# Gates of the first six tiles by a matrix product in a fused attention and mixture-of-experts kernel

## The chip, the cores and the metric

The kernel runs on one core of one Trainium2 chip. The metric is the device time of one execution in microseconds (us), the median over runs; lower is better. "The profile" is one execution taken by the hardware profiler, with the page and the trace made from it. Engines are named as there: PE does matrix products (PEld its weight loads), DVE and ACT the elementwise work, POOL the indirect transfers, and SP issues plain transfers; a q behind a name is that engine's instruction queue.

## The reference, cut to what matters

```
x   = chunked attention over q, k, v and memory rows      # 3072 tokens x 512
x   = soft mixture of experts of x                         # combine weights c (3072 x 32) times slot outputs (32 x 512)
noisy = x @ w_gate + log1p(exp(x @ w_noise)) * noise       # 3072 x 8
top2  = the two largest of noisy per token
w     = exp(top2 logits - their max) / (their sum + 1e-9)
out = zeros
for e in range(8):                                         # 512 -> 1024 -> 512
    out[tokens of e] += w[token, e] * (relu(x[tokens] @ w1[e]) @ w2[e])
```

## The kernel before

The kernel has three parts in one program. **Attention** (`attention`) and the soft experts' product (`soft`) run first; `soft` ends with the 32 x 512 slot outputs `po`, copied to SBUF as `so` (one half by ACT, one by DVE), transposed to `SOT`. **The last part** (`experts`) never forms x itself: a token's x is its row of combine weights times the slot outputs, so a gathered row of `table` (DRAM, 72 columns: 64 with the split combine weights, 8 with the token's gate for each expert) stands for a token, and the first layer of expert e is one matrix `G[e]` (128 x 1024), made by `prep_gs` from `SOT` and w1[e]. The second layer's weights are split into f16 high and low parts by `prep_hi` (ACT) and `prep_lo` (DVE), scaled by factors from `prep_s`, which need a maximum over w2[e] (`bound`, `bound_s`) and over the first layer (`prep_gmax`, `prep_row`, `prep_all`).

Tokens are worked in tiles of 128, six tiles per expert (`T0` = 6, `NTL` = 48), so tiles 0 to 5 are expert 0. For tile i:

- `gather(i)` (POOL, indirect): 128 rows of `table`, by the token indices `idx[:, i]`, into `CG[i]`
- `ct(i)`: transpose on PE and copy by ACT; `l1(i)`: eight matmuls, then HI = relu as f16 (ACT) and, by `lo(i)`, the remainder LO (DVE)
- `l2(i, ...)`: three groups of eight 128x512 matmuls, named by a number: 0 is HI with high weights, 2 is HI with low weights, 1 is LO with high weights
- `gate(i)`, `yv(i)`: the gate GW and the scaled copy y out of PSUM (ACT); `put(i)`: y is added to the rows of `out` by an indirect transfer on POOL

Indices of expert 0 are made first, by an early count of its tokens: a mask `s0`, its prefix sums, then `spread` builds the one-hot `oh_0` (24 blocks, 128 x 128 f16) and `ov` (block numbers times token values), and `inverse` multiplies them (24 matmuls) to `pv0`, which `decode` turns into `idx[:, 0:6]`. The other experts' indices follow later from all counts (`bases`, `positions`, `columns`, `invert`). Gates come from the top-2 choice (`top_max`, `top_eq`, `top_oh`: one-hots `oh`; `d`: difference of the two logits; `w12`: the two weights; `wd`: token by expert). As tiles 0 to 5 are gathered before `wd` exists, `wd` goes to a second DRAM table `gtab` as well, and `gates(i)` gathers from that; tiles 0 and 1 are copied from PSUM unscaled and multiplied in place by `rescale`.

`out` is cleared by four transfers of a quarter each (`zeros`), issued by SP; `load_e(1, 0)` and `load_e(1, 1)` load w1 and w2 of expert 1 (2 MB each, four transfers). All plain transfers named here go through SP's queue in the order in which they are written.

The order on each engine is the program order, written by hand. After the ramp (tiles 0 and 1, lines 703 to 808) a loop over `seq` does tile n, with the first layer of tile n+1 ahead of the second layer of tile n, and with the preparation of the next expert spread over the tiles by `plan`, `mid` and `ahead`.

Of the kernel before, what the change touches and what calls it, by code (L numbers as in the profile page):

```python
# [9 lines left out]
F32 = mybir.dt.float32  # L10
# [4 lines left out]
OP = mybir.AluOpType  # L15
# [110 lines left out]
def tile_kernel(ctx, tc, q, k, v, mem_k, mem_v, phi, sw1, sw2, wg, wn, noise, mw1, mw2, cf_in, c16_in, out):  # L126
# [9 lines left out]
    table = dr.tile([N + ND, ROW], F32, name="table")  # L136
    gtab = dr.tile([N + ND, E], F32, name="gtab")
    bp = ctx.enter_context(tc.tile_pool(name="bp", bufs=1))
# [5 lines left out]
    with ExitStack() as sctx:  # L144
# [44 lines left out]
        with ExitStack() as fctx:  # L189
            fw = fctx.enter_context(tc.tile_pool(name="fw", bufs=1))  # L190
            ft = fctx.enter_context(tc.tile_pool(name="ft", bufs=1, side="right"))
            tabs = [ft.tile([128, NT // 2, ROW], F32, name=f"tab{z}") for z in range(2)]
            ps = fctx.enter_context(tc.tile_pool(name="ps2", bufs=1, space=PSUM))
            for m in range(4, 11):
                for x in range(4):
                    load_w(m, x)

            def next_load(m, x):
                if 2 <= m < 7:
                    load_w(m + 9, x)  # L200

            rw = [t.rearrange("p (k d) -> p k d", k=n) for t, n in zip(raw, (4, 8))]

            def first_load():
                for t, src in ((rw[1], mw2), (rw[0], mw1)):
                    n = t.shape[1]
                    for x in range(4):
                        k = slice(x * n // 4, (x + 1) * n // 4)
                        nc.sync.dma_start(t[:, k, :], src[0].rearrange("(j p) f -> p j f", p=128)[:, k, :])

            def bounds():
                first_load()
                bound(nc, rw, big, s4, 0)
                bound(nc, rw, big, s4, 1, True)

            soft(tc, nc, phis, L, C, CT, SOT, zt, table, gtab, K, WT, next_load, bounds, tabs, fw, ps)
    with ExitStack() as ectx:
        rt = ectx.enter_context(tc.tile_pool(name="rt", bufs=1))
        ew = ectx.enter_context(tc.tile_pool(name="ew", bufs=2))
        ps = ectx.enter_context(tc.tile_pool(name="ps3", bufs=1, space=PSUM))  # L220
        experts(tc, nc, C, CT, SOT, sog, wgn, nz, zt, table, gtab, mw1, mw2, out, K, K16, rw, s4, big, rt, ew, ps)

# [16 lines left out]
def soft(tc, nc, SIT, L, C, CT, SOT, zt, table, gtab, K, WT, next_load, first_load, tabs, fw, ps):  # L239
    identf = K["ident"]  # L240
# [55 lines left out]
    for z in range(2):  # L296
        nc.sync.dma_start(table[z * N // 2:(z + 1) * N // 2].rearrange("(t p) c -> p t c", p=128), wrs[z])
    for t, w in ((table, ROW), (gtab, E)):
        nc.sync.dma_start(t[N:N + ND].rearrange("(t p) c -> p t c", p=128),
                          zt[:, None, 0:w].to_broadcast([128, ND // 128, w]))  # L300
    so = fw.tile([128, DM], F32, name="so")
    nc.scalar.activation(so[:, :DM // 2], po[:, :DM // 2], AF.Copy)
    nc.vector.tensor_copy(so[:, DM // 2:], po[:, DM // 2:])
    pt = ps.tile([128, 4, SL], F32, name="pd", bufs=1)
    for j in range(4):
# [3 lines left out]

def experts(tc, nc, C, CT, SOT, sog, wgn, nz, zt, table, gtab, mw1, mw2, out, K, K16, rw, s4, big, rt, ew, ps):  # L310
    spare = C.rearrange("p t s -> p (t s)")[:, F // 2:]
# [253 lines left out]
    prep_all(0, 0, 1)  # L565
    top_max(1)
    prep_s(0, 0, 1)
    for x in range(4):
        prep_hi(0, x)

    CG, CTT, HI, LO, RG, GT, GG, GW, YV, P2, PI = ({} for _ in range(11))

    def gather(i):
        CG[i] = ew.tile([128, ROW], F32, name="cg", bufs=7)
        c = GCOL(i)
        nc.gpsimd.indirect_dma_start(out=CG[i], out_offset=None, in_=table,  # L576
                                     in_offset=bass.IndirectOffsetOnAxis(ap=idx[:, c:c + 1], axis=0))

    def gates(i):
        GG[i] = ew.tile([128, 8], F32, name="gg", bufs=3)  # L580
        nc.gpsimd.indirect_dma_start(out=GG[i], out_offset=None, in_=gtab,
                                     in_offset=bass.IndirectOffsetOnAxis(ap=idx[:, i:i + 1], axis=0))
# [147 lines left out]
    nc.vector.reciprocal(w12[:, 0], w12[:, 0])  # L730
    tt(w12[:, 1], w12[:, 0], d, OP.mult)
# [639 lines left out]
```

## Time and profile before

| | |
|---|---|
| median of 3 runs | 554.92 us (554.15 to 556.75) |
| the profiled execution | 553.13 us, its span 551.3 us |
| PE busy | 483.7 us, 88% of the span |
| DVE, ACT, POOL busy | 324.3, 262.0, 258.3 us (59%, 48%, 47%) |
| chain that ended last | PE 67%, of it 40% line 666 (`l2`) |
| DMA | 111.34 MB, 202 GB/s over the span |

The span runs from the first to the last instruction that the profile holds. The part that the diff touches begins near 194 us, when the last matmuls of `soft` end, and reaches to about 275 us, when the loop over tiles has its regular rhythm.

### The profile page before, as it was taken

Reading aid. Unit: us, or ns where it says so; the run is one execution under the profiler, and the core shown is the slowest. Engines: PE = TensorE matmul, PEld = TensorE weight load, DVE = VectorE, ACT = ScalarE, POOL = GpSimd, SP = SyncE. Lnnn points to the kernel's source line nnn. Section 1 sums busy time; section 2 is a strip of 40 time slices with the busy share of each in tenths; the row PEclk is TensorE's granted clock in tenths of the full one; section 3 lists DMA queues with packets and bytes.
Section 4 is the critical chain, followed back from the end, with each engine's and each line's share of the span. In section 5 each row is a group of like instructions: output and inputs, shape, how many; then the busy total and the mean of one; then the engine's idle time right before and its main releaser. Section 6 shows DMA issues by size and latency. Waiting matters only on the chain.

```text
span 551.3 us, 12206 instructions
## 1 busy us (share of the span) xinstructions
PE 483.7 (88%) x4781; PEld 268.3 (49%) x4781; DVE 324.3 (59%) x725; ACT 262.0 (48%) x460; POOL 258.3 (47%) x312
## 2 busy tenths in 40 slices
PE   4799999997878872959899999999999999999990
PEld 3667667664424341424444454445544544545540
DVE  6799999999622046667656656563584565642110
ACT  4888888882112052236625346264272552642310
POOL 5988878781030004035733636355335464463241
PEclk9999999999999965898999999999999999999996
DMA  8799998869999999974593966748757673344352
GB/s 194 201 252 236 245 241 227 228 206 358 413 357 410 411 339 372 272 306 60 122 281 45 270 143 198 197 68 200 191 152 166 161 200 48 45 60 63 39 65 36
DMA packets 90161, 111.34 MB, mean 202 GB/s; under 512 B 43392, under 2 KB 55840, under 8 KB 90096
## 3 DMA queue, kind: packets, MB, share of 16 engines
q1 hardware_dynamic: 76944, 94.03, 53.6%
q0 software_dynamic: 9648, 16.20, 20.0%
q10 hardware_dynamic: 3504, 0.25, 0.5%
q8 instruction: 40, 0.66, 0.5%
q14 instruction: 25, 0.20, 0.1%
HBM read 89.21 MB, written 21.25 MB: 200 GB/s over the span
## 4 chain that ended last, share of the span: by engine, by line
PE 67%; ACT 8%; DMA 8%; issue 6%; DVE 5%; POOL 3%; ACTq 0%; POOLq 0%; DVEq 0%
PE l L666 40%; ACT big L1041 4%; PE tr L1031 4%; PE st L1055 4%; PE l L638 3%; DMA out_dram<-y,C 3%; PE av L1101 2%; PE g L369 2%; DMA w<-in_moe_w_dram 2%; DMA big<-in_moe_w_dram 2%; PE po L267 1%; PE p L253 1%; PE xt L1124 1%; ACT qT L1041 1%; PE xt L1138 1%
## 5 line engine op out<-in xcount | busy, mean ns | idle before, releaser
L666 PE MATMUL l<-big,hi 128*128 128x512 f16 x768 | 175.7, 381 | 0.1
L692 POOL DMA_INDIRECT out_dram<-y,C x52 | 87.6, 1685 | 140.7 <-ACT ctt L600 90.8
L648 DVE SCALAR_TENSOR_TENSOR lo<-l,hi 128x1024 f16<-128x1024 f32 x50 | 61.2, 1224 | 116.6 <-ACT hi L640 109.2
L666 PEld LDWEIGHTS <-hi 128*128 128x128 f16 x768 | 72.8, 98 | 84.2 <-issue 4.8
L683 ACT ACTIVATE y<-l,gw 128x512 f32<-128x512 f32 x48 | 32.8, 684 | 144.9 <-PE l L666 136.9
L666 PE MATMUL l<-big,lo 128*128 128x512 f16 x384 | 92.2, 383 | 0.0
L576 POOL DMA_INDIRECT cg<-table,C x50 | 54.2, 1085 | 48.4 <-DVE big L531 29.0
L666 PEld LDWEIGHTS <-lo 128*128 128x128 f16 x384 | 37.9, 99 | 45.0 <-issue 1.6
L1008 POOL COPY big<-big 32x768 f32<-32x768 f32 x64 | 56.5, 882 | 3.7
L640 ACT ACTIVATE hi<-l 128x1024 f16<-128x1024 f32 x50 | 51.2, 1024 | 3.5 <-issue 1.8
L1041 ACT ACTIVATE qT<-tr 64x384 f32<-64x384 f32 x64 | 34.3, 536 | 13.5 <-PE tr L1031 12.9
L433 DVE SCALAR_TENSOR_TENSOR big<-w,C,big 128x1024 f16<-128x1024 f32 x32 | 39.9, 1279 | 1.3 <-issue 1.1
L1031 PE MATMUL tr<-cf,big 128*128 128x128 f32 x192 | 30.3, 298 | 7.6 <-DMA cf<-in_const_f_dram 4.5
L429 ACT ACTIVATE big<-w,C 128x1024 f16<-128x1024 f32 x32 | 35.4, 1148 | 0.9 <-DVE C L405 0.7
L1041 ACT ACTIVATE big<-tr 64x384 f32<-64x384 f32 x64 | 32.9, 514 | 4.8 <-PE tr L1031 3.9
L1055 PE MATMUL st<-big,qT 128*32 128x128 f32 (+2 forms) x768 | 28.5, 284 | 5.1 <-ACT big L1041 3.2
L638 PE MATMUL l<-ctt,big 128*128 128x128 f16 x384 | 29.7, 221 | 3.0 <-ACT ctt L600 2.6
L1101 PE MATMUL av<-big,aT 128*32 128x130 f32 x768 | 27.9, 278 | 3.3 <-PE at L1086 2.1
L1013 POOL COPY big<-big 24x768 f32<-24x768 f32 x32 | 26.3, 824 | 9.5 <-DMA big<-in_v_dram 8.2
L1031 PEld LDWEIGHTS tr<-cf,big 128*128 128x128 f32 x192 | 22.2, 149 | 14.1 <-DMA cf<-in_const_f_dram 4.5
L638 PEld LDWEIGHTS <-big 128*128 128x128 f16 x384 | 23.9, 99 | 9.7 <-issue 4.5
L381 DVE TENSOR_REDUCE mxp<-w 128x1 f32<-128x2048 f32 x12 | 27.3, 2277 | 0.0
(247 smaller groups left out, 601.4 us busy)
## 6 DMA issues: line engine op xcount, KB each, us to landing
w<-in_moe_w_dram SPq DMA_DIRECT2D x72, 512.0 KB, 7.7
big<-in_moe_w_dram SPq DMA_DIRECT2D x56, 512.0 KB, 9.5
big<-in_v_dram SPq DMA_DIRECT2D x62, 104.0 KB, 4.7
big<-in_q_dram SPq DMA_DIRECT2D x16, 384.0 KB, 3.7
big<-in_k_dram SPq DMA_DIRECT2D x16, 384.0 KB, 6.0
out_dram<-zt SPq DMA_DIRECT2D x4, 1536.0 KB, 11.4
table<-tab SPq DMA_DIRECT2D x2, 432.0 KB
out_dram<-y,C POOLq DMA_INDIRECT x52
```

Source lines behind the costliest of these rows:

```text
L433: stt(lo, w2, sc[:, rk, 5:6], hi, op0=OP.mult, op1=OP.subtract)
L576: nc.gpsimd.indirect_dma_start(out=CG[i], out_offset=None, in_=table, in_offset=bass.IndirectOffsetOnAxis(ap=idx[:, c:c + 1], axis=0))
L638: nc.tensor.matmul(p[:, k, :], GT[i][:, 128 * k:128 * k + 128], CTT[i], start=True, stop=True)
L640: nc.scalar.activation(HI[i], p, AF.Relu)
L648: stt(LO[i].rearrange("p k t -> p (k t)"), p.rearrange("p k t -> p (k t)"), 0.0, HI[i].rearrange("p k t -> p (k t)"), op0=OP.max, op1=OP.s ...
L666: nc.tensor.matmul(P2[i], h[i][:, k, :], dyn(W2f, i, w * 4096 + 512 * k, 512, RG.get(i)), start=x == 0 and k == 0, stop=x == last and k == 7)
L692: b = nc.gpsimd.indirect_dma_start(out=out, out_offset=bass.IndirectOffsetOnAxis(ap=idx[:, c:c + 1], axis=0), in_=y, in_offset=None, compu ...
L1008: nc.gpsimd.tensor_copy(vcols(i, p, 32, 66 * h, D), mvs[p:p + 32, i // 2:i // 2 + 1, :].to_broadcast([32, NH, D]))
L1031: nc.tensor.transpose(p[:, y, 128 * t:128 * t + 128], RW[n % 3][:, 128 * i:128 * i + 128], identf)
L1041: nc.scalar.activation(o, i, AF.Copy)
L1055: nc.tensor.matmul(st[32 * j:32 * j + 32, g, :, w0:w1], QT[u][:, 32 * c:32 * c + 32], kb[:, :, 40 * c + w0:40 * c + w1], start=True, stop= ...
L1101: nc.tensor.matmul(p[32 * j:32 * j + 32, g, :], AT[i][:, g, 32 * j:32 * j + 32], VB[i % NV][:, c:c + 130], start=True, stop=True, tile_pos ...
```

## The change

- `gtab`, its clearing, its writing from `wd` and the six gathers from it are gone. In their place the gates of tiles 0 to 5 come from a matrix product: `weights0` (DVE, six operations) splits the tokens' weights for expert 0 into two f16 parts `w16` and multiplies the one-hot block numbers `ot` (now kept) by them to `ow`; `gates0` multiplies `oh_0` by `ow` (24 matmuls, 12 columns), and two DVE operations sum and scale to `gw0` (128 x 6).
- Tiles 0 and 1 are scaled when they are copied out of PSUM; `rescale` and `ready` are gone; `put(0)` and `put(1)` stand ahead of the loop.
- Before the first gathers SP has one quarter of the clearing; the first transfer of `load_e(1, 0)` waits for gathers 0 and 1 to land, and the other three quarters stand behind it.
- The order of the ramp: the two bounds of w2[0] that stood ahead of the `so` copies stand behind them (ACT's) and behind the logits' matmuls (DVE's); `prep_s(0, 1, 2)` stands behind the mask `s0`; `d`, its exponential and `w12` stand around the gathers; `wd` and its write to `table` stand behind the last `prep_lo(0, ...)`; `ct(2)` and `l1(2)` stand ahead of `l2(1, (1,))`; `lo(2)` stands between `positions` and `columns`.

```diff
-    gtab = dr.tile([N + ND, E], F32, name="gtab")
...
             def bounds():
-                first_load()
                 bound(nc, rw, big, s4, 0)
-                bound(nc, rw, big, s4, 1, True)
...
     first_load()
...
-    for t, w in ((table, ROW), (gtab, E)):
-        nc.sync.dma_start(t[N:N + ND].rearrange("(t p) c -> p t c", p=128),
-                          zt[:, None, 0:w].to_broadcast([128, ND // 128, w]))
+    nc.sync.dma_start(table[N:N + ND].rearrange("(t p) c -> p t c", p=128),
+                      zt[:, None, 0:ROW].to_broadcast([128, ND // 128, ROW]))
...
     nc.vector.tensor_copy(so[:, DM // 2:], po[:, DM // 2:])
+    bounds()
...
     for x in range(2, 4):
         bound_s(x)
+    bound(nc, rw, big, s4, 1, True)
     vt(sc[:, 0, 1:2], s4, AX.X, OP.max)
...
-    prep_s(0, 1, 2)
...
+    prep_s(0, 1, 2)
     top_max(0)
...
-    spread(ov, K16["t0"], t0, 0, NT)
-    tt(ov, ov, bc(val0[:, :, None], NT, T0), OP.mult)
+    ot = T(NT, T0, dt=F16)
+    spread(ot, K16["t0"], t0, 0, NT)
+    tt(ov, ot, bc(val0[:, :, None], NT, T0), OP.mult)
...
     top_max(1)
+    d = T(NT)
+    tt(d, m[:, 1], m[:, 0], OP.subtract)
     prep_s(0, 0, 1)
     for x in range(4):
         prep_hi(0, x)
+    nc.scalar.activation(d, d, AF.Exp)
...
-    for i in range(T0):
-        gather(i)
+    first = [gather(i) for i in range(T0)]
+    w12 = T(2, NT)
+    ts(w12[:, 0], d, 1.0, 1.0e-9, op0=OP.add, op1=OP.add)
+    nc.vector.reciprocal(w12[:, 0], w12[:, 0])
+    tt(w12[:, 1], w12[:, 0], d, OP.mult)
     top_eq(1)
     prep_gs(0)
     top_oh(1)
...
+    def weights0():
+        tt(w0, oh[:, :, :, 0], w12, OP.mult)
+        tt(w0[:, 0], w0[:, 0], w0[:, 1], OP.add)
+        ts(w16[:, 0], w0[:, 0], 1024.0, None, op0=OP.mult)
+        stt(w16[:, 1], w0[:, 0], 1024.0, w16[:, 0], op0=OP.mult, op1=OP.subtract)
+        for x in range(2):
+            tt(ow[:, :, x], ot, bc(w16[:, x, :, None], NT, T0), OP.mult)
+
+    def gates0():
+        p = ps.tile([128, 2, T0], F32, name="g", bufs=1)
+        for j in range(NT):
+            nc.tensor.matmul(p.rearrange("p x s -> p (x s)"), oh_0[:, j, :], ow[:, j].rearrange("p x s -> p (x s)"),
+                             start=j == 0, stop=j == NT - 1)
+        vt(gw0, p.rearrange("p x s -> p s x"), AX.X, OP.add)
+        ts(gw0, gw0, sc[:, 0, 6:7], 2.0 ** -10, op0=OP.mult, op1=OP.mult)
...
-    zeros(0, 2)
-    load_e(1, 0)
-    zeros(2, NZ)
+    zeros(0, 1)
+    after = load_e(1, 0)
+    for x in first[:2]:
+        tc.add_manual_dep(after, x.name, mybir.DependencyInfo(mybir.DependencyClass.Sync, mybir.DependencyReason.DATA),
+                          reason="bulk transfers behind the first gathers")
+    zeros(1, NZ)
     ct(0)
     l1(0, False)
...
-    ts(w12[:, 0], d, 1.0, 1.0e-9, op0=OP.add, op1=OP.add)
...
+    weights0()
     lo(0)
-    for k in range(2):
-        tt(wx[:, k], oh[:, k], bc(w12[:, k, :, None], NT, E), OP.mult)
-    tt(wd, wx[:, 0], wx[:, 1], OP.add)
-    nc.scalar.dma_start(gtab[0:N].rearrange("(t p) c -> p t c", p=128), wd)
-    nc.sync.dma_start(table[0:N, 64:ROW].rearrange("(t p) c -> p t c", p=128), wd)
     prep_inv(0)
     l2(0, (0,), 2)
     ct(1)
...
     lo(1)
+    gates0()
     l2(1, (0,), 2)
     prep_lo(0, 2)
     prep_lo(0, 3)
+    for k in range(2):
+        tt(wx[:, k], oh[:, k], bc(w12[:, k, :, None], NT, E), OP.mult)
+    tt(wd, wx[:, 0], wx[:, 1], OP.add)
+    nc.sync.dma_start(table[0:N, 64:ROW].rearrange("(t p) c -> p t c", p=128), wd)
     load_e(1, 1)
+    gate(0)
+    gate(1)
     l2(0, (2,), 2)
-    yv(0, False)
+    yv(0)
+    ct(2)
+    l1(2, False)
     l2(1, (1,), 2)
-    ct(2)
-    l1(2)
     ct(3)
     l2(1, (2,), 2)
-    yv(1, False)
+    yv(1)
...
     bases()
     positions()
-    gates(0)
-    gates(1)
-    gates(2)
+    lo(2)
     columns(0)
     columns(1)
+    put(0)
+    put(1)
...
-        if n < 3:
-            for x in range(3):
-                ready(x) if x < 2 else gate(x)
-        else:
-            gate(i)
+        gate(i)
...
-        if n == 2:
-            put(0)
-            gates(3)
-            put(1)
-            gates(4)
-            gates(5)
```

## Rows read from the trace of the kernel before

**Rows 1.** Stretches: start:end, length, busy time (count) by engine, PEclk, DMA share, GB/s.

```profile
211.00:219.00 8.00, 0.00 (x0) 0.00 (x0) 5.86 (x28) 2.13 (x5) 4.96 (x5) 0.50 1.06 389
...
242.50:249.10 6.60, 0.00 (x0) 0.00 (x0) 4.14 (x10) 3.99 (x7) 2.67 (x3) 0.72 0.89 311
...
275.00:511.00 236.00, 236.00 (x1611) 118.65 (x1599) 130.07 (x208) 106.01 (x170) 111.39 (x117) 1.00 0.62 146
```

**Rows 2.** Timeline to the first gather: start, length, instruction [idle before <- releaser].

```profile
193.61 0.60 PE L267 MATMUL po<-big,hz 128*32 128x512 f32 x2
...
195.66 1.22 DVE L234 TENSOR_REDUCE s<-w 128x1 f32<-128x1024 f32 x1 [4.21 <-DMA w<-in_moe_w_dram]
196.80 0.41 DVE L303 COPY so<-po 128x256 f32<-128x256 f32 x1
...
197.27 0.77 PE L306 MATMUL pd<-cf,so 128*128 128x32 f32 x4 [0.69 <-DVE so L303]
...
203.59 0.43 DVE L511 TENSOR_TENSOR big<-big,nz 128x96 f32<-128x96 f32 x2
...
211.64 0.17 DVE L475 SCALAR_TENSOR_TENSOR C<-ct,big 128x6 int32<-128x6 f32 x1
...
212.82 1.04 POOL L576 DMA_INDIRECT cg<-table,C  x1 [29.00 <-DVE big L531]
```

**Rows 3.** Timeline from the first gather to the first tile.

```profile
215.98 0.42 DVE L421 COPY big<-big 32x1024 f16<-32x1024 f16 x1
...
219.06 0.29 PE L598 MATMUL ct<-c,cg 128*128 128x128 f16 x1 [8.48 <-DMA cg<-table,C]
...
219.77 1.01 PE L638 MATMUL l<-ctt,big 128*128 128x128 f16 x8 [0.41 <-issue]
...
222.12 0.18 DVE L729 TENSOR_SCALAR big<-big 128x24 f32<-128x24 f32 x1 [0.68 <-ACT big L726]
```

**Rows 4.** DMA busy tenths in 40 slices of 261 to 268 us; a gather there.

```profile
DMA  0000000000004300000430000056000004800000
...
261.46 0.99 POOL L576 DMA_INDIRECT cg<-table,C  x1 [4.80 <-DVE C L815]
```

**Rows 5.** Groups by line and form, 194 to 262 us: xcount | busy us, mean ns.

```profile
L648 DVE SCALAR_TENSOR_TENSOR lo<-l,hi 128x1024 f16<-128x1024 f32 x5 | 6.1, 1223 | 9.1 <-ACT hi L640 9.1
...
L457 DVE TENSOR_TENSOR big<-c,ns 128x3072 f16<-128x3072 f16 x2 | 3.4, 1750 | 0.0
...
L683 ACT ACTIVATE y<-l,gw 128x512 f32<-128x512 f32 x2 | 1.4, 677 | 3.0 <-PE l L666 3.0
...
L375 DVE TENSOR_REDUCE C<-g 128x1 f32<-128x256 f32 x2 | 0.8, 416 | 0.0
...
L734 DVE TENSOR_TENSOR big<-big 128x192 f32<-128x192 f32 x2 | 0.6, 351 | 0.0
```

**Rows 6.** Timeline of tiles 0 to 3.

```profile
221.89 3.38 PE L666 MATMUL l<-big,hi 128*128 128x512 f16 x8
...
228.84 2.47 DVE L433 SCALAR_TENSOR_TENSOR big<-w,C,big 128x1024 f16<-128x1024 f32 x2
...
234.67 1.89 PE L666 MATMUL l<-big,hi 128*128 128x512 f16 x8
...
237.07 0.16 DVE L762 TENSOR_SCALAR big<-big 128x8 f32<-128x8 f32 x1
...
242.01 0.73 DVE L457 TENSOR_TENSOR big<-c,tq 128x1104 f16<-128x1104 f16 x1
...
249.13 0.37 PE L390 MATMUL g<-cf,C 128*1 128x128 f32 x1 [6.64 <-DVE C L375]
...
258.41 1.37 PE L467 MATMUL ct<-big 128*128 128x46 f16 x48
```

**Rows 7.** Waits of SP's queue, 200 to 250 us; transfers: KB each, us to landing.

```profile
SPq L442 <- DMA gtab<-big: 8.7, 1, 8.7
...
out_dram<-zt SPq DMA_DIRECT2D x4, 1536.0 KB, 11.4
```

More of the change, by code (lines that the diff above doesn't have):

```diff
@@ L211, in bounds @@
             def bounds():
-                first_load()
                 bound(nc, rw, big, s4, 0)
-                bound(nc, rw, big, s4, 1, True)
-            soft(tc, nc, phis, L, C, CT, SOT, zt, table, gtab, K, WT, next_load, bounds, tabs, fw, ps)
+            soft(tc, nc, phis, L, C, CT, SOT, zt, table, K, WT, next_load, first_load, bounds, tabs, fw, ps)
     with ExitStack() as ectx:
@@ L220, in tile_kernel @@
         ps = ectx.enter_context(tc.tile_pool(name="ps3", bufs=1, space=PSUM))
-        experts(tc, nc, C, CT, SOT, sog, wgn, nz, zt, table, gtab, mw1, mw2, out, K, K16, rw, s4, big, rt, ew, ps)
+        experts(tc, nc, C, CT, SOT, sog, wgn, nz, zt, table, mw1, mw2, out, K, K16, rw, s4, big, rt, ew, ps)
 def zero_out(q, out, zt, x):
@@ L236, in bound, with soft @@
         nc.scalar.activation(big[:, 6144:7168], w, AF.Abs, accum_out=s4[:, x:x + 1])
-def soft(tc, nc, SIT, L, C, CT, SOT, zt, table, gtab, K, WT, next_load, first_load, tabs, fw, ps):
+def soft(tc, nc, SIT, L, C, CT, SOT, zt, table, K, WT, next_load, first_load, bounds, tabs, fw, ps):
     identf = K["ident"]
@@ L307, in soft, with experts @@
     nc.vector.tensor_copy(SOT, pt)
-def experts(tc, nc, C, CT, SOT, sog, wgn, nz, zt, table, gtab, mw1, mw2, out, K, K16, rw, s4, big, rt, ew, ps):
+def experts(tc, nc, C, CT, SOT, sog, wgn, nz, zt, table, mw1, mw2, out, K, K16, rw, s4, big, rt, ew, ps):
     spare = C.rearrange("p t s -> p (t s)")[:, F // 2:]
@@ L439, in load_e @@
         src, n = ((mw1, 4), (mw2, 8))[which]
+        out = []
         for x in parts or range(4):
             k = slice(x * n // 4, (x + 1) * n // 4)
-            nc.sync.dma_start(rw[which][:, k, :], src[rk].rearrange("(j p) f -> p j f", p=128)[:, k, :])
+            b = nc.sync.dma_start(rw[which][:, k, :], src[rk].rearrange("(j p) f -> p j f", p=128)[:, k, :])
+            out.append(b.ins)
+        return out[0]
     BIG = 1.5 * 2.0 ** 30
@@ L569, in experts @@
         prep_hi(0, x)
-    CG, CTT, HI, LO, RG, GT, GG, GW, YV, P2, PI = ({} for _ in range(11))
+    nc.scalar.activation(d, d, AF.Exp)
+    CG, CTT, HI, LO, RG, GT, GW, YV, P2, PI = ({} for _ in range(10))
     def gather(i):
@@ L575, in gather @@
         c = GCOL(i)
[L576 to L582, printed above, removed]
-    for i in range(T0):
-        gather(i)
+        b = nc.gpsimd.indirect_dma_start(out=CG[i], out_offset=None, in_=table,
+                                         in_offset=bass.IndirectOffsetOnAxis(ap=idx[:, c:c + 1], axis=0))
+        return b.ins
+    first = [gather(i) for i in range(T0)]
[3 more added lines that the diff above has]
+    tt(w12[:, 1], w12[:, 0], d, OP.mult)
     top_eq(1)
@@ L592, in experts @@
     ohb = ohb.rearrange("p t e -> p (t e)")
-    d = T(NT)
-    tt(d, m[:, 1], m[:, 0], OP.subtract)
+    w0 = T(2, NT)
+    w16 = T(2, NT, dt=F16)
+    ow = T(NT, 2, T0, dt=F16)
+    gw0 = T(T0)
+    def weights0():
[12 more added lines that the diff above has]
+        ts(gw0, gw0, sc[:, 0, 6:7], 2.0 ** -10, op0=OP.mult, op1=OP.mult)
     def ct(i):
@@ L669, in gate @@
     def gate(i):
-        GW[i] = ew.tile([128, 1], F32, name="gw", bufs=3)
+        if i < T0:
+            GW[i] = gw0[:, i:i + 1]
+            return
+        GW[i] = ew.tile([128, 1], F32, name="gw")
         if i < NTL:
             e = i // T0
-            w = GG[i][:, 0:1] if i < T0 else CG[i][:, 64 + e:65 + e]
-            tt(GW[i], w, sc[:, e, 6:7], OP.mult)
+            tt(GW[i], CG[i][:, 64 + e:65 + e], sc[:, e, 6:7], OP.mult)
             return
@@ L679, in gate, with yv @@
         stt(scr, scr, 1.0, msk, op0=OP.mult, op1=OP.mult, accum_out=GW[i])
-    def yv(i, scaled=True):
+    def yv(i):
         YV[i] = ew.tile([128, DM], F32, name="y", bufs=4)
-        nc.scalar.activation(YV[i], P2.pop(i), AF.Copy, scale=GW.pop(i) if scaled else 1.0)
-    def rescale(i):
-        nc.scalar.activation(YV[i], YV[i], AF.Copy, scale=GW.pop(i))
+        nc.scalar.activation(YV[i], P2.pop(i), AF.Copy, scale=GW.pop(i))
     def put(i):
@@ L720, in experts @@
     nc.tensor.matmul(pq, K16["u"], ohb, start=False, stop=True)
-    w12 = T(2, NT)
     wx = T(2, NT, E)
@@ L725, in experts @@
     cnt = T(E)
-    nc.scalar.activation(d, d, AF.Exp)
     nc.scalar.activation(pp.rearrange("p t e -> p (t e)"), pq, AF.Copy)
     vt(cnt, pn.rearrange("p (t e) -> p e t", e=E), AX.X, OP.add)
-    ts(w12[:, 0], d, 1.0, 1.0e-9, op0=OP.add, op1=OP.add)
-    nc.vector.reciprocal(w12[:, 0], w12[:, 0])
-    tt(w12[:, 1], w12[:, 0], d, OP.mult)
+    weights0()
     lo(0)
-    for k in range(2):
-        tt(wx[:, k], oh[:, k], bc(w12[:, k, :, None], NT, E), OP.mult)
-    tt(wd, wx[:, 0], wx[:, 1], OP.add)
-    nc.scalar.dma_start(gtab[0:N].rearrange("(t p) c -> p t c", p=128), wd)
-    nc.sync.dma_start(table[0:N, 64:ROW].rearrange("(t p) c -> p t c", p=128), wd)
     prep_inv(0)
@@ L803, in experts @@
     positions()
-    gates(0)
-    gates(1)
-    gates(2)
+    lo(2)
     columns(0)
     columns(1)
-    def ready(i):
-        gate(i)
-        rescale(i)
+    put(0)
+    put(1)
     def max1():
@@ L869, in experts @@
             gather(seq[n + 6])
-        if n < 3:
-            for x in range(3):
-                ready(x) if x < 2 else gate(x)
-        else:
-            gate(i)
+        gate(i)
         for f, *a in AHEAD.get(n, ()):
```

## The prediction

> **What bounds the kernel now.** I read the stretches first, then the waits of PE, then the timeline around each of them. From 275 to 511 us PE is busy for 236.00 of 236.00 us at the full clock [rows 1]: the rhythm over the tiles is PE's alone, so an earlier start of it comes out at the end, and nothing that DVE, ACT or the queues do there counts. What can be won lies in the ramp between 194 and 253 us. The reader is to see two holes of PE there: 8.48 us before 219.06, ended by the landing of the first gather, and 6.64 us before 249.13, ended by `prep_gmax` (L375) on DVE [rows 3, 6]; PE's busy time in these stretches is zero [rows 1]. A third thing is the chain of small steps from the soft experts to the indices, which starts late because DVE's copy of `so` stands behind a bound that waits for weights [rows 2].
>
> **The head, up to the indices.** PE's last product ends at 193.61 + 0.60 = 194.21. DVE's half of `so` starts only at 196.80, after the bound L234, which waited 4.21 us for its load [rows 2]. With the bounds moved, both halves start at 194.25, and DVE's ends at 194.7. The second four matmuls of `pd` then follow the first four instead of starting at 197.27; if the first take between 0.6 and these 0.77 us, they start at 195.3 to 195.5, so the chain is 1.8 to 2.0 earlier. I take 2.0. DVE's bound (1.22) then runs while PE makes the logits (L487), and ACT's bounds end no later, since they wait for the same loads; without that cover it would cost 1.22. The three operations of `prep_s(0, 1, 2)`, each about as long as L729's 0.18 [rows 3], leave the way to L511 and come back behind `s0`, on the way to the indices: the noisy logits are 2.5 us earlier, the indices (L475, ending at 211.81) 2.0, at 209.8.
>
> **The first gather.** It started 1.0 us after the indices [rows 2]. The trace does not say whether that second is POOL's own or the landing of `table`. If it is POOL's, the gather starts at 210.8; if it is the table, it stays near 212.8. At 261.46 the same instruction followed its indices at once, with no such second [rows 4], which leaves both open; I take 210.8, and the end of the instruction at 211.85. Before, from its end at 212.82 + 1.04 = 213.86 to PE's transpose it took 5.2 us, with the DMA engines full (share 1.06) [rows 1, 3]. In a quiet stretch a gather ended at 262.45, and its bytes moved in the 13th and 14th slices of 0.175 us, 263.1 to 263.5, so it had landed about 1.1 us after its end [rows 4]. After the change one quarter of the clearing, 1536 KB [rows 7] or 1.57 MB, is ahead: at 389 GB/s [rows 1] that is 4.0 us, over near 212.5 if it follows the table as now. So the gather meets some traffic and then none: bounds 1.1 and 5.2, I take 2.0, since the queue is empty 0.7 us after the gather's end, and the landing at 213.9.
>
> The Trainium skill, "DMA: Bandwidth & Descriptors", section "Queues, rings and completion order", says that each DMA engine takes turns between the queues that have work, a packet at a time; by that the full SP queue should hardly delay a gather, and the wait would do nothing. The trace speaks against it with its 5.2 against 1.1 us, but these are two stretches that differ in more than the queue. What follows if the rule holds stands below as the second rival.
>
> **The first tile.** It also needs `G[0]`, whose last piece DVE wrote at 215.98 + 0.42 = 216.40 [rows 3]. That comes 2.0 earlier, less one operation for `d` (0.2) and three for `w12` (at 0.18 to 0.3 like L729, together 0.7) that now stand ahead of it: 215.3. The gather at 213.9 and its transpose and copy (0.7 from 219.06 to 219.77) are ready by 214.6, so `l1(0)` starts at 215.3 instead of 219.77: 4.5 us. DVE, not the gather, is late next; a landing up to 214.6 costs nothing.
>
> **Tiles 0 and 1.** All of it moves 4.5 us. Added on PE: `gates0`, 24 matmuls; 48 of the same kind with wider columns took 1.37 us [rows 6], so 0.7. Moved: `yv(0)`, 0.68 us on ACT [rows 5], now stands ahead of the copy for `ct(2)`, for which PE waits; I count 0.5 of it, bounds 0 and 0.7. `weights0`, four operations of 0.18 and two of about 0.3 (between L729 and L734), is 1.3 us of DVE ahead of `lo(0)`. It is hidden: `lo(0)` feeds only the LO group, which comes after eight matmuls of 3.38 us [rows 6] and the whole first layer of tile 1; uncovered it would cost the 1.3. Tile 1 ended at 234.67 + 1.89 = 236.56 and ends at 236.6 - 4.5 + 1.2 = 233.3. The eight matmuls take 3.38 us at the low clock and 1.89 at the full one [rows 6]; if the clock rose at the same moment as now, not as long after the first of them, up to eight more would be slow: 1.5 us, and part of it is covered by DVE below.
>
> **DVE from there, and the second hole.** `prep_lo` ended at 228.84 + 2.47 = 231.31 [rows 6]. Moved 4.5, with two gate operations (0.4) and a wait for `gates0` (0.4): 227.6. Then `wd`, three operations of 0.35 [rows 5]: 228.65. `bases` and `positions` took 242.01 - 237.07 = 4.9 [rows 6]; they began so late because `lo(2)` stood ahead of them and waited for ACT. Now they need only counts: 233.6. `lo(2)` 1.22 [rows 5]: 234.8, its input long there. `columns`, four of 0.73 [rows 6]: 237.7. `lo(3)` 1.22 and `prep_gmax` 0.42 [rows 5]: 239.4. In the kernel before, `lo(3)` waited in addition for ACT, which stood at `rescale` until the gates were gathered and scaled (9.1 us of waiting for HI in five of them [rows 5]); that is gone. PE reaches its transpose (L390) after tile 1 and the 5.9 us that it had between 236.56 and the hole: 239.25. So 0.15 us of the 6.64 stay, and L390 starts at 239.4 instead of 249.13: 9.7 earlier. The eight LO matmuls behind it run at the full clock, 1.5 us less, but PE then needs the maximum that DVE takes behind the two `spread`s of 1.75 [rows 5], at 239.4 + 3.5 + 0.3 = 243.2, where PE would be at 242.3: most of the 1.5 goes back. I count 0.15 of it. Sum: 9.7 + 0.15, about 9.9 us at tile 3, and from there PE has the same work in the same order.
>
> **SP and POOL.** Behind the wait on SP stand the three other quarters of the clearing, the write of `wd` and `load_e(1, 1)`. Nobody needs the clearing before `put(0)`. It ends later: 2.1 + 4.7 MB from about 216 at 389 GB/s is 17.5 us, 233.5, and POOL's `put(0)` waits for that with nothing behind it but gathers whose indices come at 251. `load_e(1, 1)` is issued near 229 rather than after 8.7 us of waiting behind `gtab` [rows 7], queues behind the clearing and the write, and lands by about 241; ACT's `bound_s` of its last piece stands behind tile 3's `prep_gs`, by my sum near 247. So 6 us cover it.
>
> **The sum.** The profiled execution took 553.13 us, 1.8 outside its span, and 9.9 less is 543.2. The median of the runs, 554.92, is 1.8 above that execution; less 9.9 it is 545.0, which I predict.
>
> **The rivals.** *The hold does nothing for the gather* (the rule above, or a wait that is not where I think). Gather 0 then lands 5.2 after its end, 217.0, and `l1(0)` starts at 217.7: 2.4 less, the rest of the chain moves with it, some 7.5 won, 547.4. For it: the quarter ahead is still draining when the gather is issued. Against: 1.1 in quiet. *DVE becomes the bound of the ramp*: between 215 and 243 my sum leaves DVE hardly an idle us, and PE meets it at 239.3 and 242.3. Each us by which an added operation, or a `lo` waiting for ACT, is longer comes out whole. With 4 us more of that, 6 are won: 549. For it: the margin is 0.15 us; against: every operation on it but the small new ones has a row. *Slower*: the transfers that are held move right, and w2[1] comes late. Up to a landing at 247 that is free, from there each us is paid, since bound, scale, `prep_hi` and tile 6 hang on it; it takes all of the gain when the last piece lands after 257, and at 259 the kernel is 2 slower, 557. For it: DMA share 1.06 until the ramp's tiles, and the additions of `put(0)` and `put(1)` now meet these loads. Against: the queue empties by 241 by its rate, 16 us before.
>
> **How the numbers follow.** My forecast, 542.5 to 547 with 545.0 the likeliest: 0.70. The hold without effect: 0.12. DVE as the bound: 0.11. Won less than 0.5% (2.8 us, about what a measurement here can tell) because several terms fail: 0.04. Slower: 0.03. Faster is the first three, 0.93. The range takes the first two and DVE's case to 549.5, and down to 542.5, where the clock would stay up through the head: 542.5 to 549.5.
>
> **What would show it.** Right: L511 near 201, first gather near 211, its transpose 2 to 3 us after its end, `l1(0)` near 215.3, no hole above 1 us before L390, which starts near 239.4. Wrong: the first gather still at 212.8 or landing 5 us after its end; PE waiting for L375 or L391 for some us; SP's `load_e(1, 1)` or ACT's `bound_s` on a landing after 247; or a low clock again between 225 and 253.

## The result: 541.5 us, 2.4% faster, and the profile after

The kernel with the change takes 541.5 us in the median (540.3 to 543.7), the kernel before in the same session 555.2 (554.2 to 556.8): ratio 0.976, 95% interval 0.972 to 0.980. The forecast was 545.0, with a range of 542.5 to 549.5, so the kernel is a good 3 us faster than forecast and 1 us below the range. Three single executions among the runs below, at 602, 990 and 1681 us, count in no median or ratio. The profiled execution took 542.2 us, 10.9 less than the profiled one before, with a span of 540.3.

The two traces can't be laid over each other from their start: the last product of the soft experts ended at 194.21 in the one and ends at 194.31 + 1.92 = 196.23 in the other, though nothing ahead of it was changed. Over the fourteen profiled executions of this study it ended between 194.2 and 197.6. So **all distances below are counted from the end of that product** ("behind `po`"), which each trace shows as its last row of `po`.

The timeline of the kernel after, from the head to tile 6 (start, length, engine, line, operation; idle time before it and what ended it):

```profile
194.31 1.92 PE L264 MATMUL po<-big,hz 128*32 128x512 f32 x16 [0.35 <-DVE hz L260]
196.72 0.42 DVE L299 COPY so<-po 128x256 f32<-128x256 f32 x1 [2.46 <-ACT so L298]
198.88 1.21 DVE L231 TENSOR_REDUCE s<-w 128x1 f32<-128x1024 f32 x1
199.01 1.55 PE L487 MATMUL l<-sog,CT 128*128 128x64 f32 x12 [0.36 <-DVE sog L484]
200.85 0.16 DVE L495 TENSOR_REDUCE C<-s 128x1 f32<-128x4 f32 x1 [0.77 <-ACT big L233]
201.68 0.41 DVE L511 TENSOR_TENSOR big<-big,nz 128x96 f32<-128x96 f32 x2
210.19 0.17 DVE L475 SCALAR_TENSOR_TENSOR C<-ct,big 128x6 int32<-128x6 f32 x1
211.37 1.04 POOL L581 DMA_INDIRECT cg<-table,C  x1 [24.74 <-DVE C L402]
214.05 0.29 PE L620 MATMUL ct<-c,cg 128*128 128x128 f16 x1 [4.92 <-DMA cg<-table,C]
215.21 0.42 DVE L418 COPY big<-big 32x1024 f16<-32x1024 f16 x1
215.77 1.01 PE L660 MATMUL l<-ctt,big 128*128 128x128 f16 x8 [1.44 <-DVE big L418]
224.11 0.75 PE L613 MATMUL g<-big 128*128 128x12 f16 x24
231.52 1.89 PE L688 MATMUL l<-big,hi 128*128 128x512 f16 x8
238.44 0.41 DVE L372 TENSOR_REDUCE C<-g 128x1 f32<-128x256 f32 x1
239.17 0.27 PE L387 MATMUL g<-cf,C 128*1 128x128 f32 x1
239.28 1.89 PE L688 MATMUL l<-big,lo 128*128 128x512 f16 x8
242.44 0.21 PE L393 MATMUL g<-cf,mxr 1*128 1x1 f32 x1 [0.76 <-DVE mxr L388]
260.55 0.61 PE L660 MATMUL l<-ctt,big 128*128 128x128 f16 x8 [1.48 <-ACT ctt L622]
```

The idle time in PE's row at 214.05 is the first hole: it was 8.48 us [rows 3] and is 4.92, and PE then waits 1.44 more for DVE's last piece of `G`, which is late next, as forecast. In the head DVE waits 0.77 us at L495 for ACT's last bound of w2[0] (L233): that bound now stands between the logits and the indices. The row at 239.17 (L387 is the old L390) has no idle time in front of it: the second hole of 6.64 us [rows 6] is gone. The stretches (length, busy time of PE, PEld, DVE, ACT, POOL, granted clock, DMA share, GB/s) show the rest:

```profile
196.24:199.00 2.76, 1.53 (x40) 1.33 (x40) 0.98 (x4) 2.09 (x4) 0.00 (x0) 1.00 1.05 414
199.00:200.60 1.60, 1.55 (x12) 1.42 (x12) 1.08 (x1) 1.40 (x3) 0.00 (x0) 1.00 1.05 428
200.60:203.00 2.40, 1.56 (x14) 0.80 (x18) 1.68 (x10) 0.80 (x4) 0.00 (x0) 0.57 1.03 403
214.00:221.40 7.40, 5.85 (x24) 2.80 (x25) 6.75 (x22) 1.63 (x3) 4.11 (x5) 0.50 0.71 221
221.40:239.20 17.80, 16.55 (x142) 8.61 (x141) 16.02 (x36) 5.22 (x9) 0.30 (x1) 1.00 1.03 311
239.20:242.60 3.40, 2.64 (x21) 1.50 (x20) 3.18 (x3) 0.85 (x1) 3.13 (x3) 1.00 0.86 316
264.00:500.00 236.00, 236.00 (x1610) 118.60 (x1608) 129.90 (x208) 106.20 (x170) 112.36 (x119) 1.00 0.63 147
```

The rhythm over the tiles is PE's alone as before (236.00 of 236.00). The clock is at the full level until the logits (199.00 to 200.60) are through, falls behind them, is at half in the first tile, and from 221.4 on is full; a second fall, which the kernel before had around its second hole, does not come.

The change behind `po`, with a second profiled execution of the same kernel (`a0_after`) and the forecast (us gained):

| event | before | after | second | gained | forecast |
|---|---|---|---|---|---|
| logits' last product | 8.0 | 4.3 | 4.6 | 3.7, 3.4 | 2.0 |
| indices (L475) written | 17.6 | 14.1 | 14.7 | 3.5, 2.9 | 2.0 |
| `l1(0)` starts | 25.6 | 19.5 | 20.1 | 6.0, 5.4 | 4.5 |
| tile 1 ends | 42.4 | 37.2 | 37.0 | 5.2, 5.3 | 3.3 |
| L390, after: L387 | 54.9 | 42.9 | 42.8 | 12.0, 12.1 | 9.7 |
| end of the span | 357.1 | 344.1 | 344.4 | 13.0, 12.7 | 9.9 |

For the second execution I had expected, on record before it ran, 344 to 345 us from `po` to the end and the logits again at 1.55 us and done 4.3 behind `po`. The end came as expected. The logits took longer, since the clock fell while they ran (0.78 over 199.20 to 201.10), and DVE then waited 1.48 us at L495 rather than 0.77:

```profile
199.20 1.89 PE L487 MATMUL l<-sog,CT 128*128 128x64 f32 x12 [0.36 <-DVE sog L484]
```

### The profile page after: what moved, and what is told of

It is laid out like the page before. It is cut to its first block, busy times and chain, and to the rows that moved or that the text cites. A ratio compares the mean times of both kernels' runs of the same rounds, so it can differ in the third digit from the quotient of the medians.

```text
span 540.3 us, 12253 instructions
## 1 busy us (share of the span) xinstructions
PE 482.4 (89%) x4805; PEld 267.3 (49%) x4805; DVE 325.4 (60%) x727; ACT 260.4 (48%) x458; POOL 252.6 (47%) x306
## 4 chain that ended last, share of the span: by engine, by line
PE 64%; ACT 10%; DMA 10%; DVE 7%; issue 4%; POOL 3%; SPq 1%; POOLq 0%; DVEq 0%; ACTq 0%
PE l L688 41%; DMA big<-in_moe_w_dram 5%; PE l L660 4%; ACT big L1049 3%; PE tr L1039 3%; DMA w<-in_moe_w_dram 3%; PE st L1063 3%; PE g L366 2%; PE l L685 2%; PE av L1109 2%; ACT qT L1049 2%; PE po L264 1%; PE xt L1132 1%; DVE big L1021 1%; DMA big<-in_q_dram 1%
## 5 line engine op out<-in xcount | busy, mean ns | idle before, releaser
L707 ACT ACTIVATE y<-l,gw 128x512 f32<-128x512 f32 x44 | 30.1, 684 | 138.3 <-PE l L688 133.4
L688 PE MATMUL l<-big,lo 128*128 128x512 f16 x384 | 90.7, 379 | 0.0
L581 POOL DMA_INDIRECT cg<-table,C x50 | 53.0, 1061 | 45.6 <-DVE C L402 24.7
L1049 ACT ACTIVATE qT<-tr 64x384 f32<-64x384 f32 x64 | 34.1, 534 | 13.1 <-PE tr L1039 12.5
L1021 POOL COPY big<-big 24x768 f32<-24x768 f32 x32 | 27.6, 863 | 7.7 <-DMA big<-in_v_dram 6.3
L1039 PEld LDWEIGHTS tr<-cf,big 128*128 128x128 f32 x192 | 22.2, 149 | 14.0 <-issue 4.5
```

What stands on the lines that cost most here:

```text
L581: b = nc.gpsimd.indirect_dma_start(out=CG[i], out_offset=None, in_=table, in_offset=bass.IndirectOffsetOnAxis(ap=idx[:, c:c + 1], axis=0))
L688: nc.tensor.matmul(P2[i], h[i][:, k, :], dyn(W2f, i, w * 4096 + 512 * k, 512, RG.get(i)), start=x == 0 and k == 0, stop=x == last and k == 7)
L1039: nc.tensor.transpose(p[:, y, 128 * t:128 * t + 128], RW[n % 3][:, 128 * i:128 * i + 128], identf)
L1049: nc.scalar.activation(o, i, AF.Copy)
```

## The experiments

Theory: the 13 us come from the three places of the forecast, which stand in series, and all were priced too low, the head most. Rivals: the hold does nothing (packets of several queues take turns), or one part alone makes nearly all of the gain. The first four runs undo one part of the change each. Medians stand beside the kernel before on the same chip (554.4, later 554.0 and 553.9).

**The hold undone.**

```diff
-    zeros(0, 1)
-    after = load_e(1, 0)
-    for x in first[:2]:
-        tc.add_manual_dep(after, x.name, ...)
-    zeros(1, NZ)
+    zeros(0, 2)
+    load_e(1, 0)
+    zeros(2, NZ)
```

> The changed kernel, with the hold alone undone: two quarters of the clearing, expert 1's w1 and the other two quarters are issued at once, as before. Theory A (a full queue delays the gather): the first gather lands 4 to 5 us after its end instead of 1.6, PE's transpose comes some 3 us later, and with the 1.4 us that it now waits for G[0] the first layer of tile 0 starts 2 us later; DVE's chain moves with it, and the end by 1.5 to 2.5, near 543.5. Rival B (the DMA engines take the queues in turn, so the gather never waited for the bulk): landing within 2.5 us of its end, first layer where it is, end unchanged within 0.5.

Measured: 544.5 us, ratio 0.981 (0.977 to 0.985). The timeline of this kernel:

```profile
192.62 3.10 PE L264 MATMUL po<-big,hz 128*32 128x512 f32 x16 [0.35 <-DVE hz L260]
211.55 1.04 POOL L581 DMA_INDIRECT cg<-table,C  x1 [26.61 <-DVE C L402]
218.40 0.29 PE L620 MATMUL ct<-c,cg 128*128 128x128 f16 x1 [9.08 <-DMA cg<-table,C]
```

From the end of the gather's instruction (212.59) to PE's transpose it is 5.8 us; in the kernel after it is 214.05 - 212.41 = 1.6. The stretch between the two, in the kernel after and then in this one:

```profile
212.40:214.05 1.65, 0.00 (x0) 0.00 (x1) 1.48 (x5) 1.22 (x3) 1.04 (x3) 0.50 0.34 89
212.60:218.40 5.80, 0.00 (x0) 0.00 (x1) 3.98 (x14) 1.20 (x3) 4.29 (x5) 0.50 1.06 382
```

The DMA engines' share is 0.34 there with the hold and 1.06 without it. The span ends 543.2 - 195.72 = 347.5 behind `po` instead of 344.1. The hold is worth 3.4 us, against 2.4 in the forecast (545.0 against its rival's 547.4) and the 1.5 to 2.5 expected here, and the rival falls.

**The head undone** (the bounds ahead of the `so` copies again, `prep_s(0, 1, 2)` in its old place).

```diff
                 bound(nc, rw, big, s4, 0)
+                bound(nc, rw, big, s4, 1, True)
...
+    bounds()
     nc.scalar.activation(so[:, :DM // 2], po[:, :DM // 2], AF.Copy)
     nc.vector.tensor_copy(so[:, DM // 2:], po[:, DM // 2:])
-    bounds()
...
-    bound(nc, rw, big, s4, 1, True)
...
+    prep_s(0, 1, 2)
     nc.scalar.activation(az, z, AF.Exp)
```

> The changed kernel, with the old head: the bounds of w2[0] ahead of the so copies and prep_s(0, 1, 2) ahead of the noisy logits. Theory A: the indices come 3.5 us later, counted from PE's last product of the soft experts (17.6 instead of 14.1), all behind them moves with it, end 2.5 to 3.5 later, near 544.5; of it 1.3 is TensorE's clock, the twelve matmuls of the logits taking 2.8 instead of 1.55 us. Rival B (as the prediction had it): 2.0 later and 2 at the end, the logits at 1.55 or 2.8 alike in both orders. Rival C: the tile's start hangs on something else, below 1.

Measured: 544.5 us, ratio 0.982 (0.978 to 0.985). The timeline, and the two stretches before and of the logits:

```profile
192.27 2.50 PE L265 MATMUL po<-big,hz 128*32 128x512 f32 x16 [0.35 <-DVE hz L261]
199.64 2.82 PE L488 MATMUL l<-sog,CT 128*128 128x64 f32 x12 [0.35 <-DVE sog L485]
213.07 1.04 POOL L581 DMA_INDIRECT cg<-table,C  x1 [28.48 <-DVE C L403]
```

```profile
194.77:199.64 4.87, 1.71 (x40) 1.39 (x40) 2.07 (x4) 3.31 (x6) 0.00 (x0) 0.95 1.04 417
199.64:202.47 2.83, 2.83 (x13) 2.64 (x13) 0.16 (x1) 0.41 (x2) 0.00 (x0) 0.50 1.06 387
```

Here the logits start 4.9 behind `po` instead of 2.8, after the clock has fallen, and take 2.82 us instead of 1.55. The span ends 542.3 - 194.77 = 347.5 behind `po`: the head is worth 3.4 us here (3.2 against the second execution). At the logits' end 2.1 us are the earlier start and 1.3 the clock. Not all of that reaches the indices, since DVE waits behind the logits for ACT's bound: they come 17.3 behind `po`, against 14.1 and 14.7. How much of the 3.4 us is the clock's own share is not shown.

**`lo(2)` in its old place**, ahead of `bases` and `positions`.

```diff
-    l1(2, False)
+    l1(2)
...
     positions()
-    lo(2)
     columns(0)
```

> The changed kernel, with lo(2) back ahead of bases and positions. Theory A (DVE's order sets when the maximum for expert 1 is ready): bases start only behind HI and LO of tile 2, some 3.7 us later, less the 1.2 of lo(2) that is then behind; PE stands before the transpose L387 for about 2.5 us and the end moves by 2 to 2.5. Rival B (DVE has slack there): no hole, end unchanged.

Measured: 544.6 us, ratio 0.981 (0.976 to 0.986). The timeline, behind one row of the kernel before, where `lo(2)` stands in the same place:

```profile
235.93 1.22 DVE L648 SCALAR_TENSOR_TENSOR lo<-l,hi 128x1024 f16<-128x1024 f32 x1 [4.61 <-ACT hi L640]
```

```profile
230.87 1.22 DVE L670 SCALAR_TENSOR_TENSOR lo<-l,hi 128x1024 f16<-128x1024 f32 x1 [2.42 <-ACT hi L662]
232.01 0.16 DVE L784 TENSOR_SCALAR big<-big 128x8 f32<-128x8 f32 x1
241.36 0.27 PE L387 MATMUL g<-cf,C 128*1 128x128 f32 x1 [2.20 <-DVE C L372]
```

DVE stands 2.42 us at `lo(2)` waiting for ACT (4.61 in the kernel before), and a hole of 2.20 us opens before L387. The span ends 542.8 - 196.32 = 346.5 behind `po`, 2.4 later, as expected: what DVE loses comes out whole.

**The gates from the table again**, in a kernel with the new head, the hold and the new place of `lo(2)`. As short diff, against the kernel before, all but the head and the hold (above) that changes:

```diff
-    l1(2)
+    l1(2, False)
...
     gates(2)
+    lo(2)
     columns(0)
```

> The kernel before with the new head, the hold and the place of lo(2), but with the gates still from the second table and by gathers, and with rescale. Theory A (the gates' way through DRAM is what made the second hole): the table's rows land only behind the held clearing, near 236 to 238, three gathers later DVE has the gates near 244, and PE stands 5 to 7 us before the transpose for expert 1; end 5 to 6.5 later than the changed kernel, near 547. Rival B (the order alone made the hole): within 1 of the changed kernel.

Measured: 552.3 us, ratio 0.996 (0.994 to 0.999); the span ends 549.0 - 195.13 = 353.9 behind `po`, 9.8 later than after where I had expected 5 to 6.5. The timeline, and the stretch of its second hole:

```profile
220.06 0.39 ACTq L742 DMA_DIRECT2D gtab<-big  x1
236.96 0.94 POOL L585 DMA_INDIRECT gg<-gtab,C  x1 [18.30 <-issue]
241.63 0.37 DVE L677 TENSOR_TENSOR gw<-gg,C 128x1 f32<-128x1 f32 x2 [6.73 <-DMA gg<-gtab,C]
246.17 0.37 PE L389 MATMUL g<-cf,C 128*1 128x128 f32 x1 [8.86 <-DVE C L374]
```

```profile
240.40:250.70 10.30, 4.53 (x18) 2.18 (x18) 5.47 (x8) 5.30 (x10) 6.87 (x6) 0.50 1.00 345
```

`gtab` is written at 220.06, but the first gather from it starts 16.9 us later; DVE then waits 6.73 for it, and PE 8.86. The clock is at half from 240.4 to 250.7, through the hole and the products behind it, which I had not counted. With the table path 9.8 of the 13.0 us are gone: 8.1 at L389 (51.0 behind `po` instead of 42.9), where the later landing is what DVE waits for, and the rest behind it. The kernel with the head and `lo(2)`, the table, and no hold was not tried; part of the 9.8 us may be the hold's, which puts the clearing beside the table's write.

**One part alone.** The next three put single parts into the kernel before (the hold as in the first diff, reversed; the head as in the second, reversed) or keep the gates alone (the first three diffs applied to the kernel after).

> The kernel before with the hold alone. Theory A (the first two holes are in series, and the second one is set by the second table's landing behind the clearing): the first gather lands 1.3 us after its end, the first layer of tile 0 starts 3 us earlier, but the table of gates lands no earlier, PE waits at the transpose for expert 1 as long as before by the clock on the wall, and the end moves by less than 1. Rival B (holes add up): 3.4 us won, as the hold is worth in the changed kernel.

> The kernel before with the new head alone. Theory A: the indices come 2.8 us earlier (the logits at 1.55 us), the first gather still lands 5 us after its end, the first layer of tile 0 starts 3 us earlier, and the second hole eats it, since the gates' table lands when the clearing is through: end within 1. Rival B: 3.4 us won.

> The changed kernel without the hold, with the old head, and with lo(2) ahead of bases: what is left are the gates by the product and what goes with it. Theory A: the first layer of tile 0 starts where it does in the kernel before (25.6 us after PE's last product of the soft experts), the transpose for expert 1 comes 26 us behind that as in the run with lo(2) first, 3.4 earlier than before; end 3 to 4.5 us below the kernel before. Rival B: nothing without the rest, within 1.

| kernel | median | ratio | L390 behind `po` | its hole | gained at the end |
|---|---|---|---|---|---|
| hold alone | 554.4 | 1.000 (0.997 to 1.002) | 53.9 | 10.16 | 0.0 |
| head alone | 551.3 | 0.995 (0.992 to 0.998) | 52.2 | 6.7 | 2.7 |
| gates alone | 550.0 | 0.992 (0.989 to 0.995) | 51.4 | 2.2 | 3.9 |
| all three and `lo(2)` | 541.5 | 0.976 (0.972 to 0.980) | 42.9 | none | 13.0 |

Alone the parts give 6.6 us, together 13.0. Of the difference, 2.4 us are what `lo(2)` was worth above, which none of the three has, and 3.4 are the hold, which alone gave nothing. The waits and rows of "hold alone" show where its gain goes:

```profile
PE ct L601 <- DMA cg<-table,C: 4.8, 1, 4.8
PE g L390 <- DVE C L375: 10.2, 1, 10.2
```

```profile
221.97 0.39 ACTq L742 DMA_DIRECT2D gtab<-big  x1
238.81 1.47 POOL L585 DMA_INDIRECT gg<-gtab,C  x1 [18.24 <-issue]
243.38 0.16 DVE L677 TENSOR_TENSOR gw<-gg,C 128x1 f32<-128x1 f32 x1 [1.74 <-DMA gg<-gtab,C]
```

Its first hole shrinks from 8.5 to 4.8 us, as in the kernel after, and its second grows from 6.6 to 10.2. (Its indices, with the head unchanged, came 16.3 behind `po`, 1.3 earlier than in the profile of the kernel before; that gained nothing either. The 1.0 us that it leads at L390 is gone at the end.) The held clearing now runs while `gtab` is written, and its gather starts 16.8 us after the write was issued; in the kernel before it was 10.8:

```profile
224.95 0.39 ACTq L736 DMA_DIRECT2D gtab<-big  x1
235.72 0.94 POOL L581 DMA_INDIRECT gg<-gtab,C  x1 [15.18 <-issue]
244.84 0.29 DVE L674 TENSOR_TENSOR gw<-gg,C 128x1 f32<-128x1 f32 x3
```

This last row also says what the second hole hung on before: DVE came to the gates at 244.84 without waiting for them, behind `columns`, so there DVE's own order was late, not the table. "Head alone" moves DVE's chain: its indices come 2.8 us earlier, L390 and the end 2.7, so it keeps all of its gain. I had expected under 1 of it: there I was wrong.

**A busy PE behind `po`**: 16 products whose result nobody uses, put into the kernel before, to see whether PE's idle time there lets the clock fall.

```diff
+    p1 = ps.tile([128, 256], F32, name="p1", bufs=1)
+    for j in range(4):
+        for g in range(4):
+            nc.tensor.matmul(p1[32 * g:32 * g + 32, :], SIT[:, j, :], WT[2 * E - 2][...], ...)
```

> The kernel before, with 16 matmuls of no use between the last product of the soft experts and the slot outputs' transposes, where PE stood for 1.74 us. Theory A (the clock falls because PE stands there): the clock stays up for 3 us or more longer, the logits take 1.55 instead of 2.82 us, the indices come 1 us earlier. Rival B (what falls is due to the small matmuls that follow): the clock falls where it did, logits 2.82, indices up to 0.3 later. The end stays within 1 either way, by the second hole.

Measured: 555.0 us, ratio 1.001 (0.999 to 1.003). The stretches before and of the logits, first of the kernel before, then of this one:

```profile
194.21:199.40 5.19, 2.03 (x41) 1.68 (x41) 2.07 (x4) 3.63 (x7) 0.00 (x0) 0.83 1.05 420
199.40:202.20 2.80, 2.80 (x13) 2.63 (x13) 0.16 (x1) 0.09 (x1) 0.00 (x0) 0.50 1.07 379
```

```profile
194.79:199.66 4.87, 3.44 (x67) 2.13 (x57) 2.06 (x4) 3.31 (x6) 0.00 (x0) 0.98 1.05 420
199.66:202.50 2.84, 2.84 (x13) 2.64 (x13) 0.16 (x1) 0.41 (x2) 0.00 (x0) 0.50 1.10 378
```

PE is busy 3.44 of the 4.87 us instead of 2.03 of 5.19, and the clock has fallen when the logits begin, so theory A did not come true. The granted clock is 0.98 against 0.83, but that can't be put down to the added products: the kernel with the head undone has none of them, was busy 1.71 of 4.87 us, and was granted 0.95. What counts here is that the logits come early; why the clock falls there stays open.

**Can more be had?** Three kernels move what is late next: the two `spread`s behind `l2` (`v1`), `ct(6)` earlier (`v2`), both and `w12` behind `G` (`v4`).

```diff
-        if n == 2:
-            spread(oh_s, K16["ni128"], ns2, 0, NT)
-            spread(oh_s, K16["ni128"], ns2, NT, 2 * NT)
...
         l2(i, ...)
+        if n == 2:
+            ...
...
+            plan(5, ct, 6)
...
-    mid(5, ct, 6)
...
-    w12 = T(2, NT)
-    ts(w12[:, 0], d, 1.0, 1.0e-9, op0=OP.add, op1=OP.add)
...
     prep_gs(0)
     top_oh(1)
...
+    w12 = T(2, NT)
+    ts(w12[:, 0], d, 1.0, 1.0e-9, op0=OP.add, op1=OP.add)
```

> The changed kernel with the two one-hot spreads of 1.7 us behind the maximum for expert 1's first layer instead of ahead of it. Theory A (PE's 0.76 us before L393 is DVE's order alone): that wait goes to 0.4 or less, the inverse product still finds its input, end 0.5 to 0.8 earlier. Rival B (the wait moves to the inverse product or to prep_gs): nothing.

> The changed kernel with tile 6's transpose ahead of expert 1's prep_hi on ACT. Theory A (PE's 1.48 us before the first layer of tile 6 is the copy behind four prep_hi of 1.07): the wait goes, end 1.0 to 1.5 earlier. Rival B (gather 6 has not landed yet, or tile 6's second layer then waits for prep_lo): the wait moves, end unchanged or later.

> The changed kernel with both edits and w12 behind G[0], its three operations (0.7 us) no longer ahead of the first layer of tile 0. Theory A (all three waits are orders on DVE and ACT): first layer 0.6 earlier, of which little is kept since the counts' matmuls are as late as before, and 1.5 to 2.2 from the other two: end 1.5 to 2.5 below the changed kernel, near 539.5. Rival B (DVE is the bound of the ramp): below 1.

Measured, with a second measurement of the kernel after on the same chip at 541.5 (0.977, 0.974 to 0.979): 542.6 (0.978, 0.975 to 0.981), 541.8 (0.976, 0.973 to 0.979) and 541.1 (0.976, 0.973 to 0.979). The wait of 0.76 us at 242.44 goes in `v1`, and this one comes; the wait of 1.48 before tile 6 goes in `v2`, and these two come (timelines of `v1`, then of `v2`):

```profile
254.62 0.27 PE L387 MATMUL g<-cf,C 128*1 128x128 f32 x1 [1.42 <-DVE C L833]
```

```profile
257.72 0.23 PE L620 MATMUL ct<-c,cg 128*128 128x128 f16 x1 [0.74 <-DMA cg<-table,C]
265.26 0.22 PE L620 MATMUL ct<-c,cg 128*128 128x128 f16 x1 [1.63 <-ACT y L707]
```

The waits move and none of the three is measurably faster than the change itself.

## Why the prediction came out 3 us too high

The mechanism held, but for one reason given for the second hole; sizes were off, all in one direction. **The step that failed is the head's term**: "I take 2.0" for the logits and the indices. The indices came 3.5 us earlier (2.9 in the second execution). The size of this term is the least certain: over all fourteen profiles the indices lie 13.6 to 14.8 behind `po` with the new head and 16.3 to 17.6 with the old one, with medians of 14.7 and 17.3, which are 2.6 apart. The other terms below were mis-sized too, and all of them together made the 3 us.

- *The head.* The start of the logits moved 5.2 - 2.8 = 2.4 rather than 1.8 to 2.0, although DVE's half of `so` began 0.5 behind `po`, when ACT's was done, and not at once: the eight products of `pd` then ran through in 1.09 us. The logits took 1.55 us rather than 2.82 (1.89 in the second execution), since they now run before the clock falls. I had let them take as long as before, and had the full clock through the head only as the low end of the range. `prep_s` took back its half us, as forecast. ACT's bounds end no later, as forecast, but the chain now catches up with them and waits: 0.77 us at L495, 1.48 in the second execution. The experiment that undoes the head shows both parts: logits at 4.9, 2.82 long, and 3.4 us at the end.
- *The first gather.* It started 211.37 - 210.36 = 1.0 us after the indices, as before: the lag went along although the rest moved, so it is not the landing of `table`. Its transpose came 1.6 us after its end (forecast 2.0), and 5.8 with the hold undone, which cost 3.4 us of the kernel's time. The Trainium skill, "DMA: Bandwidth & Descriptors", section "Queues, rings and completion order", has the DMA engines take turns between queues packet by packet; by that the hold should have changed little, and the traces disagree. That the sharing of packets is the cause of the 5.8 was not tried by itself.
- *The first tile.* DVE's `G` is late next: right. It ended 19.4 behind `po` instead of 22.2; the 1.5 us (0.9) that the head gave more than forecast are found again at `l1(0)`.
- *Tiles 0 and 1.* Priced at 1.2 us added; 6.0 gained at `l1(0)` are 5.2 at the end of tile 1, so 0.8 added, and 0.1 in the second execution, where the clock rose 24.3 behind `po` and the first eight products of tile 0 took 2.90 us rather than 3.59. `gates0` took 0.75 (forecast 0.7). The clock is full from 221.4 on, 25.2 behind `po`; in the kernel before it was full from 224.9, at 30.7. So its rise moved 5.5 us, with the tile (6.0), and the 1.5 us that a rise at the old moment would have cost were not paid.
- *The second hole.* Forecast 0.15 us left, none is left. DVE was on time by a small margin, as the experiment with `lo(2)` shows, where 2.4 us of waiting are 2.2 us of hole. One reason given was wrong: ACT had not stood at `rescale` for the gathered gates but for DVE, which came to them late.
- *Behind it.* Forecast 0.15 us, measured 13.0 - 12.0 = 1.0 (0.6 in the second): the LO products run at 1.89 us, and only 0.76 us is lost waiting for the maximum; that is 0.7 of it, the rest comes later and is not traced.
- *The held loads.* ACT's last bounds of w2[1] began at 249.93 and 251.11 without a wait; the slower rival had no part in it.

Together: 1.5 too little at the head, 0.4 in the tiles, 0.4 at the hole and 0.8 behind it are the 3.1 us between 9.9 and 13.0. In the second execution 0.9 at the head, 1.1 in the tiles, 0.4 at the hole and 0.4 behind it make 2.8: the total repeats better than its parts. The medians say 13.7 and, in the later session, 12.5; the profiled pair says only 10.9, because in the profiled execution after `po` itself ended 2.0 later.

## What to carry to other kernels

Holes that stand in series on one engine may have to go together: one part alone can give its time to the next hole, as the hold did with all of its 3.4 us, so a part that measures as nothing may still be needed. It need not be so: the head alone kept its 2.7 us. Count from an event that the change doesn't touch when executions differ upstream by more than the terms that are to be checked. When steps move earlier, look at the granted clock of the stretch into which they move, and not only at their old durations.

## What the runs showed of the hardware

- An indirect gather of 128 rows of 72 words was with its reader 1.6 us after its instruction's end with a DMA share of 0.34, and 5.8 us with one of 1.06. The write of a table of 96 KB and the gather that followed it were apart by 10.8 us in the kernel before, by 13.5 with the head alone, and by 16.8 and 16.9 in the two kernels that hold the clearing back until then.
- The clock fell 3.4 to 5.8 us behind `po` in the fourteen profiles, and its next rise moved with the first tile when that came 6 us earlier. Twelve products took 1.55 us before the fall, 2.82 after it, and 1.83 to 2.35 where it fell while they ran.
- Executions differ by up to 3.4 us in the part before `po`, which is the same in all kernels here; behind it the kernel after, profiled twice, repeated within 0.6 at each event of the table and within 0.3 at the end.
